# RetNet attention into an ELU feed-forward on one core: four FFN1 tiles pulled into the last attention unit of the start-up, and one weight load issued earlier

## The chip, the cores and the metric

The kernel runs on one core of one Trainium2 chip. The metric is the device time of one execution in microseconds (us); the time of a kernel is the median of its runs. All times inside the kernel are read from one profiled execution.

## The reference, cut to what matters

The input is `q`, `k`, `v` of shape (8 batches, 8 heads, 576 positions, 64) and two weights, `w_in` (512 x 2048) and `w_out` (2048 x 512), all float32.

```python
scores = scale * np.matmul(q, k.transpose(0, 1, 3, 2))
gamma = 1.0 - 2.0 ** (-5.0 - np.arange(H))
Dmat = np.where(rel >= 0, gamma ** rel, 0.0)      # decay with distance, causal; no softmax
attn = np.matmul(scores * Dmat, v)                 # per batch and head
x = attn.transpose(0, 2, 1, 3).reshape(B * S, H * D)   # 4608 tokens x 512
h = x @ w_in                                       # FFN1
g = np.where(h > 0.0, h, np.exp(np.minimum(h, 0.0)) - 1.0)   # ELU
out = g @ w_out                                    # FFN2
```

## The kernel before, in words

The 4608 tokens are cut into 36 units of 128 tokens. Nine units make two sequences, so unit 4 of each nine holds the end of one sequence and the beginning of the next. The decay is split into a factor on the values (`gk`, applied by GpSimd in `scale_v`) and a factor on the output (`gx`, applied by VectorE in `put_x`), so the attention of a unit is a linear recurrence: `turn` transposes queries and keys of the unit on TensorE (8 matmuls against an identity) and copies both halves out of PSUM, one half on VectorE and one on ScalarE; `scores` makes the key-query products; `masks` applies the causal mask on VectorE; `inter` adds the contribution of the state of earlier units; `state` updates that state; `intra` multiplies the masked scores by the values; `put_x` writes the result, transposed, into the tile `xt` that FFN1 reads; `state_out` copies the state for the next unit. `product(u)` is the last five steps in one call.

Units are gathered in groups for the feed-forward part. Group 0 is units 0, 1 and 2 (384 tokens), group 1 is unit 3 alone, and later groups have up to four units (512 tokens). `ffn1(g, ft)` makes a tile of 128 hidden features by the tokens of the group: four matmuls into a PSUM bank (`ph`), then an exponential on ScalarE (`e`, line 336), a subtraction on GpSimd (`m`, line 338), and the ELU on VectorE (`g`, line 315). The last step is held back by three tiles (`late`, `finish`, `tick`) so that VectorE's queue doesn't stand still. A tile of `ph` is free for a later tile when its `g` is written. There are three such banks (`ps_h`), and every fourth tile uses a further one (`ps_m`). `ffn2` and `ffn2_cols` multiply the `g` tiles by `w_out`.

The order of work is written out by hand for the first five units (lines 401 to 493). After that a list of FFN1 and FFN2 steps is interleaved with the attention of later units by due times (lines 496 to 553). Every engine executes its own instructions strictly in the order in which this code issues them.

In the start-up, TensorE also runs dummy matmuls (`dummy(n)`, n matmuls of a zero tile with 512 columns, line 389), whose results nobody reads. Weights are loaded with a cast from float32 to bfloat16 by DMAs that GpSimd's queue issues: `w_in` in four parts of 512 features (`load_w_in(0)` to `load_w_in(3)`, line 105; four FFN1 tiles each), `w_out` as two halves of its first 256 columns (`load_w_out(0, 0, 8)` and `load_w_out(0, 8, 16)`, line 109) and one part for its last 256 columns (`load_w_out(1, 0, 16)`). The queries and keys of each unit come by the same queue (line 94). These GpSimd transfers take eight completion semaphores in turn, so that each waits on its queue for the transfer eight places ahead of it.

The start-up loop before the change:

```python
for u in range(3):
    scores(u)
    inter(u)
    masks(u)
    if u == 0:
        make_gx(1, 2, 3)
    if u < 2:
        dummy(3)
        turn(u + 1, h)
    else:
        dummy(4)
    state(u); intra(u); put_x(u); state_out(u)
    dummy((2, 8, 2)[u])
```

Of the kernel before, what the change touches and what calls it, by code (L numbers as in the profile page):

```python
# [9 lines left out]
FP32 = mybir.dt.float32  # L10
# [7 lines left out]
def kernel(  # L18
# [9 lines left out]
    nc = tc.nc  # L28
# [4 lines left out]
    P = 128  # L33
    HP = H // 2
    KJ = DM // P
# [34 lines left out]
    ps_h = ctx.enter_context(tc.tile_pool(name="ps_h", bufs=3, space=PSUM))  # L70
# [27 lines left out]
    w_in_sb = const.tile([P, KJ, DF], BF16, name="w_in_sb")  # L98
# [8 lines left out]
    def load_w_out(c, f0, f1):  # L107
        s = (slice(None), slice(f0, f1), slice(c * 256, c * 256 + 256))
        nc.gpsimd.dma_start(w_out_sb[s], w_out_v[s])
# [17 lines left out]
    for h in range(H):  # L127
        i = h % 2
# [43 lines left out]
    def scale_v(u):  # L172
        rv = raws[u]
        n = nat.tile([P, H, D], BF16, name="vn", tag="vn")
        nc.gpsimd.tensor_tensor(  # L175
            n, rv, gk[:, u % R].unsqueeze(2).to_broadcast([P, H, D]), ALU.mult
        )
        vns[u] = n

    def turn(u, bank=None):  # L180

        t = tpool.tile([P, 2, HP, P], BF16, name="qkT", tag="qkT")
        n = kns[u]
        if u < PE_TURNED:
            if bank:
                pool, tag = bank
                ps = [pool.tile([P, HP, P], BF16, name="tr", tag=tag) for c in range(2)]
            else:
                both = ps_s.tile([P, 2, 2, HP, P], BF16, name="tr", tag="sc")
                ps = [both[:, c, 0] for c in range(2)]  # L190
            for c in range(2):
                for hp in range(HP):
                    nc.tensor.transpose(ps[c][:, hp], n[:, c, 2 * hp : 2 * hp + 2].rearrange("p h d -> p (h d)"), ident)  # L193
            nc.vector.tensor_copy(t[:, 0], ps[0])
            nc.scalar.copy(t[:, 1], ps[1])  # L195
        else:
            nc.sync.dma_start_transpose(
                t.rearrange("p c h t -> p (c h) t"), n.rearrange("p c h d -> p (c h d)")
            )
        qkTs[u] = t  # L200

    def scores(u):
        t = qkTs[u]
        sc = ps_s.tile([P, 2, HP, P], FP32, name="sc", tag="sc")
        for hp in range(HP):
            for j in range(2):
                for i in range(2):
                    r = slice(i * D, (i + 1) * D)
                    nc.tensor.matmul(  # L209
                        sc[j * 64 : (j + 1) * 64, i, hp], t[r, 1, hp, j * 64 : (j + 1) * 64], t[r, 0, hp],  # L210
                        start=(hp == 0), stop=(hp == HP - 1), skip_group_check=True,
                    )
        scs[u] = sc

    def masks(u, i=None):

        if u not in pts:
            pts[u] = ppool.tile([P, 2, HP, P], BF16, name="pt", tag="pt")
        m = mask[:, 1 if u % R == 4 else 0]
        s = slice(0, 2) if i is None else slice(i, i + 1)  # L220
        nc.vector.tensor_tensor(  # L221
            pts[u][:, s].rearrange("p i h t -> p (i h) t"), scs[u][:, s].rearrange("p i h t -> p (i h) t"),
            m.unsqueeze(1).to_broadcast([P, (s.stop - s.start) * HP, P]), ALU.mult,
        )

    def inter(u):

        o = ps_o.tile([P, HP, P], FP32, name="o", tag="o")
        os_[u] = o
        r = u % R  # L230
        if r == 0:
            return
        n = 64 if r == 4 else P
        for hp in range(HP):
            for i in range(2):
                rows = slice(i * D, (i + 1) * D)
                nc.tensor.matmul(  # L237
                    o[rows, hp, :n], sbs[u][rows, hp], qkTs[u][rows, 0, hp, :n],
                    start=(hp == 0), stop=False, skip_group_check=True,
                )  # L240

    def state(u):

        r = u % R
        if r == 8:
            return
        if r in (0, 4):
            sts[0] = ps_st.tile([P, HP, D], FP32, name="st", tag="st")
        st = sts[0]
        rows = slice(64, P) if r == 4 else slice(0, P)  # L250
        for hp in range(HP):
            for i in range(2):
                h = 2 * hp + i
                nc.tensor.matmul(  # L254
                    st[i * D : (i + 1) * D, hp], kns[u][rows, 1, h], vns[u][rows, h],
                    start=(hp == 0 and r in (0, 4)), stop=(r in (3, 7)), skip_group_check=True,
                )

    def state_out(u):
        if u % R == 8:  # L260
            return
        s = ppool.tile([P, HP, D], BF16, name="sb", tag="sb")
        nc.scalar.copy(s, sts[0])  # L263
        sbs[u + 1] = s

    def intra(u):
        o = os_[u]
        for hp in range(HP):
            for i in range(2):
                h = 2 * hp + i  # L270
                nc.tensor.matmul(  # L271
                    o[i * D : (i + 1) * D, hp], vns[u][:, h], pts[u][:, i, hp],
                    start=(u % R == 0 and hp == 0), stop=(hp == HP - 1), skip_group_check=True,
                )

    xts = {}

    def put_x(u):
        g, i = group_of[u]
        if i == 0:  # L280
            xts[g] = xpool.tile([P, KJ, 512], BF16, name="xt", tag="xt")
        r = u % R
        s0 = P * r if r < 5 else 64 + P * (r - 5)
        nc.vector.tensor_tensor(  # L284
            xts[g][:, :, i * P : (i + 1) * P], os_[u], gx[:, :, s0 : s0 + P], ALU.mult
        )
# [24 lines left out]
    def finish(n=0):  # L311

        while late and late[0][0] <= slot[0] - n:
            _, gt_, ph, m, _ = late.pop(0)
            nc.vector.scalar_tensor_tensor(gt_, ph, 0.0, m, ALU.max, ALU.min)  # L315

    def tick():
        slot[0] += 1
        finish(3)

    def ffn1(g, ft, bank=None):

        n = P * len(GROUPS[g])
        pool, tag = bank or (ps_h, "ph")
        ph = pool.tile([P, 512], FP32, name="ph", tag=tag)
        tiles = 512 // n
        w = slice(0, tiles * n)
        for i in range(tiles):
            f = (ft + i) * P
            for j in range(KJ):  # L330
                nc.tensor.matmul(  # L331
                    ph[:, i * n : (i + 1) * n], w_in_sb[:, j, f : f + P], xts[g][:, j, :n],
                    start=(j == 0), stop=(j == KJ - 1), skip_group_check=True,
                )
        e = epool.tile([P, 512], FP32, name="e", tag="e")
        nc.scalar.activation(e[:, w], ph[:, w], AF.Exp)  # L336
        m = epool.tile([P, 512], BF16, name="m", tag="m")
        nc.gpsimd.tensor_scalar(m[:, w], e[:, w], -1.0, 1.0, ALU.add, ALU.mult)  # L338
        gt_ = gpool.tile([P, 512], BF16, name="g", tag="g")
        late.append((slot[0], gt_[:, w], ph[:, w], m[:, w], (g, ft)))  # L340
        for i in range(tiles):
            gts[g, ft + i] = gt_[:, i * n : (i + 1) * n]
        tick()
# [42 lines left out]
    def dummy(n, bank=(ps_m, "pm")):  # L386
        dum = bank[0].tile([P, 512], FP32, name="dum", tag=bank[1])
        for _ in range(n):
            nc.tensor.matmul(dum, warm[:, :P], warm, start=True, stop=True)  # L389

    def product(u):
        inter(u)
        state(u)
        intra(u)
        put_x(u)
        state_out(u)

    h, m = (ps_h, "ph"), (ps_m, "pm")
# [3 lines left out]
    A(kns[0][:, 0], raw0[0])  # L402
    V(kns[0][:, 1], raw0[1])
    make_gx(0)
    turn(0, h)
    scale_v(0)
    load_w_in(1)
    scale_v(1)
# [4 lines left out]
    load_w_in(3)  # L413
    load_w_out(0, 0, 8)
    load_w_out(0, 8, 16)
    dummy(2)
    for u in range(3):
        scores(u)
        inter(u)
        masks(u)  # L420
        if u == 0:
            make_gx(1, 2, 3)
        if u < 2:
            dummy(3)
            turn(u + 1, h)
        else:
            dummy(4)
        state(u)
        intra(u)
        put_x(u)  # L430
        state_out(u)
        dummy((2, 8, 2)[u])


    def f1(g, n, bank=None):
        k = 512 // (P * len(GROUPS[g]))
        ffn1(g, k * n, bank)

    o = (ps_o, "o")
    for n in range(16):  # L440
        f1(0, n, m if n % 4 == 3 else None)
        if n == 6:
            scale_v(3)
        if n == 7:
            turn(3)
            finish(1)
            dummy(3, o)
            scores(3)
            masks(3, 0)
        if n == 8:  # L450
            masks(3, 1)
        if n == 10:
            product(3)
        if n == 11:
            load_w_out(1, 0, 16)
    for n in range(4):
        f1(1, n, m if n == 3 else None)
        if n == 0:
# [127 lines left out]
```

## Time and profile before

| what | value |
|---|---|
| median of 6 runs | 318.83 us (318.6 to 319.49) |
| profiled execution, its own time | 319.14 us |
| its span, first to last instruction | 317.4 us |
| TensorE busy | 308.8 us (97%) |
| VectorE, ScalarE, GpSimd busy | 54%, 41%, 63% |
| granted TensorE clock | 0.999 |
| bytes read from and written to HBM | 36.70 MB, 9.44 MB |

The profile has one row per engine. In a timeline row the first number is the start in us from the beginning of the span, the second how long the row's instructions lasted together, then the engine (PE is TensorE, DVE VectorE, ACT ScalarE, POOL GpSimd), the line of the code, the operation and the tiles (out<-in), and how many instructions the row merges. Square brackets give the idle time of the engine ahead of the row and what ended it. Matmuls are pipelined: the end of a row overlaps the next row, so the pace is read from start to start.

### The profile page before, as it was taken

Reading aid. Unit: us, or ns where it says so; the run is one execution under the profiler, and the core shown is the slowest. Engines: PE = TensorE matmul, PEld = TensorE weight load, DVE = VectorE, ACT = ScalarE, POOL = GpSimd, SP = SyncE. Lnnn points to the kernel's source line nnn. Section 1 sums busy time; section 2 is a strip of 40 time slices with the busy share of each in tenths; the row PEclk is TensorE's granted clock in tenths of the full one; section 3 lists DMA queues with packets and bytes.
Section 4 is the critical chain, followed back from the end, with each engine's and each line's share of the span. In section 5 each row is a group of like instructions: output and inputs, shape, how many; then the busy total and the mean of one; then the engine's idle time right before and its main releaser. Section 6 shows DMA issues by size and latency. Waiting matters only on the chain.

```text
span 317.4 us, 7528 instructions
## 1 busy us (share of the span) xinstructions
PE 308.8 (97%) x3015; PEld 173.7 (55%) x3015; DVE 172.8 (54%) x279; ACT 131.3 (41%) x243; POOL 200.7 (63%) x288
## 2 busy tenths in 40 slices
PE   8899899999999999999999999999999999999995
PEld 3455888767766555555444444444444444444444
DVE  4557434658666656565566555555555555444300
ACT  4445412444543544344444444344444444344411
POOL 7956885887987777787777666776664433333300
PEclk9999999999999999999999999999999999999999
DMA  9999999997999999999999999999996200000111
GB/s 152 189 208 150 152 191 211 162 194 61 104 143 167 155 135 167 147 128 164 130 147 135 136 133 134 132 135 133 134 132 85 66 35 35 34 33 33 67 68 67
DMA packets 149235, 39.55 MB, mean 125 GB/s; under 512 B 137616, under 2 KB 145168, under 8 KB 149200
## 3 DMA queue, kind: packets, MB, share of 16 engines
q0 software_dynamic: 79264, 13.64, 57.1%
q1 hardware_dynamic: 67920, 23.14, 37.4%
q10 hardware_dynamic: 2016, 2.29, 2.3%
q8 instruction: 23, 0.38, 0.5%
q14 instruction: 12, 0.10, 0.1%
HBM read 36.70 MB, written 9.44 MB: 145 GB/s over the span
## 4 chain that ended last, share of the span: by engine, by line
PE 88%; DVE 4%; POOL 3%; DMA 2%; issue 1%; ACT 1%; POOLq 0%; DVEq 0%; ACTq 0%
PE ph L331 37%; PE pm L356 33%; PE pmh L372 5%; PE sc L209 4%; PE o L271 3%; PE st L254 2%; DMA qkn<-in_k_dram 2%; PE o L237 2%; PE tr L193 2%; DVE pt L221 1%; PE dum L389 1%; POOL m L338 1%; DVE g L315 1%; DVE xt L284 1%; POOL qkn L94 1%
## 5 line engine op out<-in xcount | busy, mean ns | idle before, releaser
L338 POOL TENSOR_SCALAR m<-e 128x512 bf16<-128x512 f32 (+1 forms) x156 | 90.7, 584 | 97.8 <-ACT e L336 95.1
L331 PE MATMUL ph<-xt,w_in_sb 128*128 128x512 bf16 (+3 forms) x832 | 145.7, 314 | 1.4 <-DVE g L315 0.9
L315 DVE SCALAR_TENSOR_TENSOR g<-ph,m 128x512 bf16<-128x512 f32 (+1 forms) x156 | 99.7, 647 | 83.5 <-POOL m L338 82.3
L336 ACT ACTIVATE e<-ph 128x512 f32<-128x512 f32 (+1 forms) x156 | 88.0, 564 | 127.3 <-PE ph L331 126.8
L356 PE MATMUL pm<-w_out_sb,g 128*128 128x512 bf16 x496 | 125.6, 379 | 0.0
L331 PEld LDWEIGHTS <-w_in_sb 128*128 128x128 bf16 x832 | 71.4, 98 | 56.4 <-issue 2.5
L356 PEld LDWEIGHTS <-g 128*128 128x128 bf16 x496 | 47.8, 98 | 53.2 <-issue 0.3
L221 DVE TENSOR_TENSOR pt<-sc,mask 128x1024 bf16<-128x1024 f32 (+1 forms) x37 | 44.0, 1192 | 20.2 <-PE sc L209 19.9
L175 POOL TENSOR_TENSOR vn<-rv,gk 128x512 bf16<-128x512 f32 x36 | 37.5, 1042 | 2.3 <-ACT qkT L195 1.2
L94 POOL DMA_DIRECT2D qkn<-in_q_dram x39 | 35.0, 898 | 0.0
L284 DVE TENSOR_TENSOR xt<-o,gx 128x512 bf16<-128x512 f32 x36 | 24.7, 685 | 16.1 <-PE o L271 16.1
L94 POOL DMA_DIRECT2D qkn<-in_k_dram x39 | 33.3, 856 | 0.1
L363 ACT COPY ot<-pm 128x512 f32<-128x512 f32 x31 | 18.1, 585 | 14.5 <-PE pm L356 14.1
L263 ACT CAST sb<-st 128x256 bf16<-128x256 f32 x32 | 11.9, 372 | 17.2 <-PE st L254 14.4
L372 PE MATMUL pmh<-w_out_sb,g 128*128 128x256 bf16 (+1 forms) x176 | 18.5, 263 | 0.2 <-DVE g L315 0.2
L209 PEld LDWEIGHTS <-qkT 64*64 64x64 bf16 x576 | 9.2, 106 | 14.3 <-issue 11.2
L372 PEld LDWEIGHTS <-g 128*128 128x128 bf16 x176 | 15.7, 98 | 2.3 <-issue 0.4
L209 PE MATMUL sc<-qkT 64*64 64x128 bf16 x576 | 15.0, 222 | 1.0 <-ACT qkT L195 0.7
L271 PE MATMUL o<-pt,vn 128*64 128x128 bf16 x288 | 14.3, 221 | 0.0
L389 PE MATMUL dum<-warm 128*128 128x512 bf16 x39 | 12.5, 458 | 1.2 <-DVE warm L120 1.2
L237 PE MATMUL o<-qkT,sb 64*64 64x128 bf16 (+1 forms) x256 | 12.3, 214 | 0.0
L195 ACT COPY qkT<-tr 128x512 bf16<-128x512 bf16 x12 | 7.0, 585 | 11.0 <-PE tr L193 4.4
(39 smaller groups left out, 80.7 us busy)
## 6 DMA issues: line engine op xcount, KB each, us to landing
rv<-in_v_dram SPq DMA_DIRECT2D x31, 256.0 KB, 5.4
out_dram<-ot SPq DMA_DIRECT2D x27, 256.0 KB, 2.4
qkn<-in_q_dram POOLq DMA_DIRECT2D x31, 128.0 KB, 5.5
qkn<-in_k_dram POOLq DMA_DIRECT2D x31, 128.0 KB, 5.4
w_in_sb<-in_moe_w_in_dram POOLq DMA_DIRECT2D x4, 512.0 KB, 9.8
out_dram<-oth ACTq DMA_DIRECT2D x9, 128.0 KB, 4.8
w_out_sb<-in_moe_w_out_dram POOLq DMA_DIRECT2D x2, 512.0 KB, 14.1
w_out_sb<-in_moe_w_out_dram POOLq DMA_DIRECT2D x1, 1024.0 KB, 10.3
```

The lines of the kernel that those rows point to most:

```text
L94: nc.gpsimd.dma_start(kns[u][p0 : p0 + n, c], (q, k)[c][b, :, s0 : s0 + n, :].rearrange("h p d -> p h d"))
L175: nc.gpsimd.tensor_tensor(n, rv, gk[:, u % R].unsqueeze(2).to_broadcast([P, H, D]), ALU.mult)
L209: nc.tensor.matmul(sc[j * 64 : (j + 1) * 64, i, hp], t[r, 1, hp, j * 64 : (j + 1) * 64], t[r, 0, hp], start=(hp == 0), stop=(hp == HP - 1) ...
L221: nc.vector.tensor_tensor(pts[u][:, s].rearrange("p i h t -> p (i h) t"), scs[u][:, s].rearrange("p i h t -> p (i h) t"), m.unsqueeze(1).t ...
L271: nc.tensor.matmul(o[i * D : (i + 1) * D, hp], vns[u][:, h], pts[u][:, i, hp], start=(u % R == 0 and hp == 0), stop=(hp == HP - 1), skip_g ...
L284: nc.vector.tensor_tensor(xts[g][:, :, i * P : (i + 1) * P], os_[u], gx[:, :, s0 : s0 + P], ALU.mult)
L315: nc.vector.scalar_tensor_tensor(gt_, ph, 0.0, m, ALU.max, ALU.min)
L331: nc.tensor.matmul(ph[:, i * n : (i + 1) * n], w_in_sb[:, j, f : f + P], xts[g][:, j, :n], start=(j == 0), stop=(j == KJ - 1), skip_group_ ...
L336: nc.scalar.activation(e[:, w], ph[:, w], AF.Exp)
L338: nc.gpsimd.tensor_scalar(m[:, w], e[:, w], -1.0, 1.0, ALU.add, ALU.mult)
L356: nc.tensor.matmul(pm, gts[g, ft][:, it * P : (it + 1) * P], w_out_sb[:, ft], start=(ft == 0), stop=(ft == NFT - 1))
L372: nc.tensor.matmul(pm, gts[g, ft][:, it * P : (it + 1) * P], w_out_sb[:, ft, c0:c1], start=(ft == 0), stop=(ft == NFT - 1),)
```

## The change

1. `turn` gets an argument by which VectorE copies the keys and ScalarE the queries, instead of the other way round. Units 0, 1 and 2 use it.
2. `load_w_out(1, 0, 16)`, which was issued after FFN1 tile 11 of group 0, is issued with the other weight loads ahead of FFN1.
3. In the start-up, `inter` of a unit moves behind the turning of the next unit. The dummies between unit 1 and the scores of unit 2 become 2 instead of 8, and the 2 ahead of FFN1 go.
4. The first four FFN1 tiles of group 0 are made in two parts. The part for units 0 and 1 (256 columns) is done around the `product` of unit 2: two tiles ahead of it, two behind. The part for unit 2 (128 columns) follows, and then the rest of each tile's work. Tile 3 takes the `ps_m` bank, as before.
5. In group 0, unit 3 is turned after tile 5 instead of tile 7, its scores stay after tile 7, the three dummies and the forced `finish(1)` between the two go, and `scale_v(3)` moves from after tile 6 to after the scores.

```diff
-    turn(0, h)
+    turn(0, h, True)
...
     load_w_out(0, 8, 16)
+    load_w_out(1, 0, 16)
     dummy(2)
-    for u in range(3):
+    for u in range(2):
         scores(u)
-        inter(u)
         masks(u)
         if u == 0:
             make_gx(1, 2, 3)
-        if u < 2:
-            dummy(3)
-            turn(u + 1, h)
-        else:
-            dummy(4)
-        state(u)
-        intra(u)
-        put_x(u)
-        state_out(u)
-        dummy((2, 8, 2)[u])
+        dummy(3)
+        turn(u + 1, h, True)
+        product(u)
+        dummy(2)
+    scores(2)
+    masks(2)
+    dummy(4)
...
-    for n in range(16):
+    for n in range(2):
+        ffn1_part(0, n, 0, 2)
+    product(2)
+    for n in range(2, 4):
+        ffn1_part(0, n, 0, 2, m if n == 3 else None)
+    for n in range(4):
+        ffn1_part(0, n, 2, 3)
+        f1(0, n)
+    for n in range(4, 16):
         f1(0, n, m if n % 4 == 3 else None)
-        if n == 6:
-            scale_v(3)
+        if n == 5:
+            turn(3)
         if n == 7:
-            turn(3)
-            finish(1)
-            dummy(3, o)
             scores(3)
             masks(3, 0)
+            scale_v(3)
         if n == 8:
             masks(3, 1)
         if n == 10:
             product(3)
-        if n == 11:
-            load_w_out(1, 0, 16)
```

The new function makes the matmuls of one tile for the units u0 to u1 of its group, and `ffn1` picks up the tile from `phs` where it is already made:

```python
def ffn1_part(g, ft, u0, u1, bank=None):
    pool, tag = bank or (ps_h, "ph")
    if (g, ft) not in phs:
        phs[g, ft] = pool.tile([P, 512], FP32, name="ph", tag=tag)
    c = slice(u0 * P, u1 * P)
    for j in range(KJ):
        nc.tensor.matmul(
            phs[g, ft][:, c], w_in_sb[:, j, ft * P : (ft + 1) * P], xts[g][:, j, c],
            start=(j == 0), stop=(j == KJ - 1), skip_group_check=True,
        )
```

More of the change, by code (lines that the diff above doesn't have):

```diff
@@ L178, in scale_v, with turn @@
         vns[u] = n
-    def turn(u, bank=None):
+    def turn(u, bank=None, keys_on_v=False):
         t = tpool.tile([P, 2, HP, P], BF16, name="qkT", tag="qkT")
         n = kns[u]
+        c_v = 1 if keys_on_v else 0
         if u < PE_TURNED:
@@ L193, in turn @@
                     nc.tensor.transpose(ps[c][:, hp], n[:, c, 2 * hp : 2 * hp + 2].rearrange("p h d -> p (h d)"), ident)
-            nc.vector.tensor_copy(t[:, 0], ps[0])
-            nc.scalar.copy(t[:, 1], ps[1])
+            nc.vector.tensor_copy(t[:, c_v], ps[c_v])
+            nc.scalar.copy(t[:, 1 - c_v], ps[1 - c_v])
         else:
@@ L319, in tick @@
         finish(3)
+    phs = {}
+    def ffn1_part(g, ft, u0, u1, bank=None):
+        pool, tag = bank or (ps_h, "ph")
+        if (g, ft) not in phs:
+            phs[g, ft] = pool.tile([P, 512], FP32, name="ph", tag=tag)
+        c = slice(u0 * P, u1 * P)
+        for j in range(KJ):
+            nc.tensor.matmul(
+                phs[g, ft][:, c], w_in_sb[:, j, ft * P : (ft + 1) * P], xts[g][:, j, c],
+                start=(j == 0), stop=(j == KJ - 1), skip_group_check=True,
+            )
     def ffn1(g, ft, bank=None):
         n = P * len(GROUPS[g])
-        pool, tag = bank or (ps_h, "ph")
-        ph = pool.tile([P, 512], FP32, name="ph", tag=tag)
         tiles = 512 // n
         w = slice(0, tiles * n)
[L328 to L334, printed above, removed]
+        if (g, ft) in phs:
+            ph = phs.pop((g, ft))
+        else:
+            pool, tag = bank or (ps_h, "ph")
+            ph = pool.tile([P, 512], FP32, name="ph", tag=tag)
+            for i in range(tiles):
+                f = (ft + i) * P
+                for j in range(KJ):
+                    nc.tensor.matmul(
+                        ph[:, i * n : (i + 1) * n], w_in_sb[:, j, f : f + P], xts[g][:, j, :n],
+                        start=(j == 0), stop=(j == KJ - 1), skip_group_check=True,
+                    )
         e = epool.tile([P, 512], FP32, name="e", tag="e")
```

## The prediction

> **What bounds the kernel now.** I read the page first, then the waits of TensorE, then its timeline over the start-up, then GpSimd's timeline and the landing times of single transfers.
>
> ```profile
> PE 308.8 (97%) x3015; PEld 173.7 (55%) x3015; DVE 172.8 (54%) x279; ACT 131.3 (41%) x243; POOL 200.7 (63%) x288
> PEclk9999999999999999999999999999999999999999
> DMA  9999999997999999999999999999996200000111
> ```
>
> TensorE is the bound. Split by stretches, it is busy for 254.20 of the 255.00 us from 57 to 312 us, and its waits there sum to 0.4 us. So a microsecond that TensorE saves before 57 us should come out at the end whole, provided that no load becomes late. The waits from 0 to 80 us and the chain's start show what can be saved:
>
> ```profile
> PE tr L193 <- DMA qkn<-in_k_dram: 1.3, 1, 1.3
> PE ph L331 <- DVE g L315: 0.9, 1, 0.9
> PE sc L209 <- ACT qkT L195: 0.7, 2, 0.5
> PE ph L331 <- DVE xt L284: 0.2, 1, 0.2
> ```
>
> ```profile
> 12.98 0.61 PE L193 MATMUL tr<-ident,qkn 128*128 128x128 bf16 x8
> ...
> 13.99 1.90 PE L389 MATMUL dum<-warm 128*128 128x512 bf16 x8
> 15.82 0.42 PE L209 MATMUL sc<-qkT 64*64 64x128 bf16 x16
> ...
> 17.92 0.61 PE L389 MATMUL dum<-warm 128*128 128x512 bf16 x2
> 18.77 5.36 PE L331 MATMUL ph<-xt,w_in_sb 128*128 128x384 bf16 x32 [0.24 <-DVE xt L284]
> 23.96 0.61 PE L193 MATMUL tr<-ident,qkn 128*128 128x128 bf16 x8
> 24.41 0.81 PE L389 MATMUL dum<-warm 128*128 128x512 bf16 x3
> 25.71 0.42 PE L209 MATMUL sc<-qkT 64*64 64x128 bf16 x16 [0.49 <-ACT qkT L195]
> ...
> 33.29 3.73 PE L331 MATMUL ph<-xt,w_in_sb 128*128 128x128 bf16 x64 [0.91 <-DVE g L315]
> ```
>
> The reader sees TensorE filling time with dummies that cover waits (8 at 13.99, 2 at 17.92, 3 at 24.41), two waits beside them, and 0.91 us at 33.29, whose cause stands in GpSimd's timeline: the issue of the last `w_out` part, in front of four `m`.
>
> ```profile
> 30.87 1.22 POOL L109 DMA_DIRECT2D w_out_sb<-in_moe_w_out_dram  x1
> 32.12 1.94 POOL L338 TENSOR_SCALAR m<-e 128x384 bf16<-128x384 f32 x4
> ```
>
> **The change part by part.** Paces from start to start: a dummy 0.216 us, an FFN1 matmul of 384 columns 0.162 us (a tile 0.65), of 256 columns 0.109 us (8 in 1.04 us of which the last one's tail is 0.17, at 71.65), of 128 columns 0.056 us.
>
> *Up to the scores of unit 2.* The swap of the copies would free unit 0's scores some 0.16 us earlier (ACT's copy takes 0.59 us, DVE's 0.42), but TensorE then waits until 10.25 us for unit 1's keys in both kernels: worth nothing; had the keys landed sooner, 0.16. With `inter(1)` moved behind it, `turn(2)` starts at about 12.6 instead of 12.98, and there meets a transfer: unit 2's keys were issued at 4.81 and landed 8.3 us later, at 13.1. So TensorE waits about 0.35 us in the middle of that turning. The keys are turned by 13.4, `product(1)` costs 0.81 to 0.9 us (28.11 to 28.92 for unit 3's), two dummies 0.43, and the scores start at 14.8, not 15.82. The six dummies removed are 1.30 us, of which 0.3 goes to the new wait and to one more change of matmul shape. Gain: 1.00.
>
> *Up to FFN1's start.* Scores and four dummies last until 16.05. `w_in(0)` was issued at 5.67 and landed 10.0 us later, at 15.7, so it is there, by 0.4 us; `put_x(1)` ends about 15.1. Two partial tiles (8 x 0.109) run to 16.9, `product(2)` to 17.8 (its mask is done at 16.5, 0.47 + 1.22 us after the scores), two more to 18.7. `put_x(2)` starts 0.26 us after the last `intra` and takes 0.69, so it ends at 18.65: it now lies under the partial tiles. The 1.74 us of FFN1 done by 18.7 put the equivalent start at 16.96, 2.14 us after the scores; it was 2.95. Gain: 0.80, which is two dummies and the wait for `xt`.
>
> *The burst.* This is what takes most of it back. The four 128-column parts last 0.22 us each, so four tiles are finished at 19.6, and all four banks are full. Tile 4 needs `g` of tile 0. Before, tile 0's last matmul was issued by 19.41, `e` began at 19.61, `m` at 20.19, `g` at 20.73 and ended at 21.28: 1.87 us. Now tile 0 is complete at 18.92, so its `g` ends at 20.79 and tile 4 starts at 20.84: TensorE stands still for 1.24 us. Behind it the chain frees a bank every 0.48 us (four `m` in 1.94), faster than the 0.65 of a tile, so it is one stall. Queued behind tile 4 are tile 5 and unit 3's turning, which are delayed with it. Loss: 1.24.
>
> *The load moved ahead.* In the order of the built instructions the last `w_out` part is the 14th GpSimd transfer in both kernels, and waits for the semaphore of the 6th, `w_in(1)`, issued at 8.65 and landed 9.7 us later, at 18.35. In the old place this cost nothing. In the new place GpSimd stands still from 17.56 to 18.35, then issues for 1.22 us: free at 19.57. The first `m` is due at 19.70, so it is hidden by 0.13 us only; each 0.1 us of landing later than 18.5 is 0.1 us more of stall. Bounds for the issue itself: 1.22 (its own row) and 1.79 (both halves of the other columns together), so 0 to 0.45 us; I take 0, by its own row. At the old place the wait of 0.91 us goes (1.07 us by starts, 32.22 to 33.29). What is late next there is `g` of tile 12, at about 30.4, when TensorE arrives at 30.45, so no new wait. Gain: 1.07. The transfer itself now directly follows the other halves, whose second landed at 32.2; the DMA engines are nearly idle from 30 to 33 us, so it should land about 39, and its first reader comes at 44.2 − 2.8 = 41.4. The halves are first read at about 34. If the transfer were late, those microseconds come off one for one. Queries and keys of units 4 and 5 keep their place behind it in the queue; SP's queue gets nothing new.
>
> *Unit 3.* Turning after tile 5 starts at 22.1; its transfers were issued at 10.53 and 11.47 and landed by 20.1. The copies are done by about 23.2, behind `e` of tile 5, and the scores come after tile 7 at 24.0: 1.30 us (24.41 to 25.71) of dummies and waiting go, less 0.1 for one more change of shape. `scale_v(3)`, one GpSimd operation of 1.04 us, now starts behind tile 7's `m` at 25.2 and ends at 26.2; `state(3)` reads it at 26.7, and the `m` of tiles 8 and 9 queued behind it free banks that TensorE wants only at 27.9. The `w_in` parts landed at 23.2 and 25.7; tiles 8 and 12 read them at 24.3 and 27.9. VectorE's two half masks before `g` of tiles 6 and 7 leave tile 10's bank free at 25.6 when wanted at 25.65, tight. Gain: 1.2.
>
> *Sum:* 1.00 + 0.80 − 1.24 + 1.07 + 1.2 = 2.83 us.
>
> **Two rules against this change.** First, granted clock: the twelve dummies at the start step by 0.427 us, the later ones by 0.216, and the clock record begins with 1.00 at 6.3 us. TensorE's longest pause since, 1.25 us at 10.25, left it there. The Trainium skill (TensorE: Matmul & The Clock Gate, HAM oscillation — how this bites in real kernels) says that pauses over about 3.4 us throttle it to half. The new pauses (0.35, 1.24) are shorter, so the row's answer is 0 loss; were a window of 3.4 us run at half pace, the loss would be 1.7 and the sum 1.1. Second, narrower matmuls: the same page (Back-to-back issue gap) gives about 81 ns for each weight load with a 128-column matmul. The trace has 64 in 3.57 us (33.29 to 36.86), 56 ns. By the rule the sixteen 128-column matmuls cost 0.4 us more, sum 2.4; I go by the row.
>
> **The rivals.**
>
> *GpSimd is held by the moved load: slower.* GpSimd writes the descriptors of its transfers into rings of limited room (the Trainium skill, DMA: Bandwidth & Descriptors, SWDGE vs HWDGE vs iDMA, has them in a part of SBUF; no row here shows how much they hold). If those of 1024 KB don't fit behind seven transfers in flight, GpSimd waits, and all sixteen `m` with it. For it: in the old place nearly everything earlier had landed. Against it: the second half at 16.65 also had seven in flight ahead of it and took its usual 0.9 us. It decides once GpSimd is free later than 19.70 + 2.83 = 22.5. Held until `w_in(2)` lands at 23.16, it issues to 24.4; TensorE is 4.7 us later, net 1.9 slower: 320.7.
>
> *The gain is given back to the transfers.* The DMA tenths read 9 until 238 us. Were loads the pace in there, the early microseconds would turn to waits: 318.8. Against: TensorE waits 0.4 us in all after 57 us, and no wait there names a load.
>
> *The clock drops once:* 317.7, as above.
>
> *The stall is smaller,* because keys or the chain come sooner than I place them: up to 3.6 us gained, 315.2.
>
> **How the numbers follow.** The profiled execution took 319.14 us, 1.74 over its span; 319.14 − 2.83 = 316.31. The median is 0.31 lower: 318.83 − 2.83 = 316.0. Forecast 0.72 (own range 315.4 to 316.9, for the tight places at 19.57, 25.6 and 41.4), smaller stall 0.10, clock 0.05, given back 0.05, GpSimd held 0.08. Faster: 0.87; no change 0.05; slower 0.08. About 0.2%, 0.6 us, is what this measurement can tell from no change. The range of 8 in 10 goes from 315.2 to 317.3.
>
> **What would show it.** Right: scores of unit 2 near 14.8 with a wait of 0.3 on its keys; no dummies after 16; one wait of about 1.2 us of `ph` for `g` near 20.8; `w_out` issued near 18.3 on GpSimd; group 1 starting near 30.4, not 33.29; nothing new after 41. Wrong: `m` starting after 19.8, a wait of `pmh` for `w_out` near 41, or half-pace matmuls after 20.

## The result and the profile after

The changed kernel takes 317.25 us (median of 16 executions, 315.62 to 318.66), the kernel before 319.09 (34 executions). The ratio is 0.9934, with a 95% interval from 0.9917 to 0.9951: 2.1 us faster by the ratio (1.6 to 2.6). The forecast was 316.0 in a range of 315.2 to 317.3. The direction held and the median lies inside the range, but only 0.05 us from its upper end; the forecast gain of 2.83 us lies outside the interval. The executions spread over 3 us where those of the kernel before mostly keep within 1.

The profiled execution took 318.24 us over a span of 316.5, so it is one of the long ones, and it shows two things that the sum did not have. The page's clock row, and TensorE's longest wait (in all, times, longest):

```profile
PEclk9998999999999999999999999999999999999999
...
PE ph L349 <- DVE g L316: 2.0, 1, 2.0
```

The wait of `ph` for `g` is the stall of the burst, forecast at 1.24 us and here 1.96. The clock row has an 8 in its fourth slice. TensorE's timeline around it:

```profile
11.97 0.87 PE L194 MATMUL tr<-ident,qkn 128*128 128x128 bf16 x8
...
14.12 0.42 PE L210 MATMUL sc<-qkT 64*64 64x128 bf16 x16
14.47 1.04 PE L407 MATMUL dum<-warm 128*128 128x512 bf16 x4
15.35 1.04 PE L331 MATMUL ph<-xt,w_in_sb 128*128 128x256 bf16 x8
...
17.13 1.94 PE L331 MATMUL ph<-xt,w_in_sb 128*128 128x256 bf16 x24
21.03 1.57 PE L349 MATMUL ph<-xt,w_in_sb 128*128 128x384 bf16 x8 [1.96 <-DVE g L316]
22.39 1.06 PE L194 MATMUL tr<-ident,qkn 128*128 128x128 bf16 x8
23.24 2.66 PE L349 MATMUL ph<-xt,w_in_sb 128*128 128x384 bf16 x8
25.83 0.42 PE L210 MATMUL sc<-qkT 64*64 64x128 bf16 x16
```

The order of steps is the forecast one. The two lines after 22.3 are at half pace: eight matmuls of 384 columns from 23.24 take 2.59 us to the next line, where the kernel before needs 1.30. The view by windows gives, for each stretch, its length, each engine's busy time with the number of its instructions (TensorE first), and the granted clock in its third number from the right:

```profile
15.35:18.93 3.58, 3.58 (x57) 3.03 (x56) 1.16 (x2) 0.87 (x3) 1.74 (x3) 1.00 1.77 204
18.93:22.25 3.32, 1.36 (x11) 0.78 (x9) 1.83 (x4) 1.46 (x4) 2.84 (x5) 1.00 1.22 207
22.25:25.66 3.41, 3.41 (x18) 1.92 (x16) 1.48 (x4) 1.74 (x4) 1.29 (x3) 0.50 1.32 206
25.66:29.06 3.40, 3.40 (x54) 1.97 (x52) 2.68 (x5) 2.08 (x5) 2.74 (x6) 1.00 1.45 195
```

One window of 3.41 us runs at 0.50, directly behind a stretch in which TensorE was busy for 1.36 of 3.32 us. The clock record of this execution begins at 5.18 us, and 5.18 + 5 x 3.413 = 22.25: the clock changes only at the edges of windows of 3.413 us that follow one another. In the profile of before the record begins at 6.33 us, in the others at 3.98 to 7.19, so where the windows fall in the program differs from one execution to the next.

GpSimd's timeline shows why the stall was longer than the chain alone makes it:

```profile
15.06 1.79 POOL L109 DMA_DIRECT2D w_out_sb<-in_moe_w_out_dram  x2
18.69 1.15 POOL L109 DMA_DIRECT2D w_out_sb<-in_moe_w_out_dram  x1 [1.84 <-DMA w_in_sb<-in_moe_w_in_dram]
19.86 1.94 POOL L356 TENSOR_SCALAR m<-e 128x384 bf16<-128x384 f32 x4
```

The moved load waits for `w_in(1)`, as read from the order of instructions, and is issued from 18.69. The `e` of tile 0 began at 18.43, so its `m` was due at 19.01 (18.43 + 0.58) and started at 19.86: 0.85 us of this execution's stall is this load, and 1.96 − 0.85 = 1.11 the burst.

The mean clock of an execution tells whether it had such a window: 3.4 of 316 us at half pace make a mean of 0.9946. Of the changed kernel, 7 of 16 executions have a mean of 0.995 or less, with a median of 317.96; the other 9 have a median of 316.54. Of all executions of the kernel before that ran beside the experiments, 14 of 59 have such a mean, with a median of 320.66; the other 45 have 319.09. At full clock the change is therefore worth 319.09 − 316.54 = 2.55 us, give or take a few tenths: the nine executions go from 315.62 to 318.28.

### The profile page after: what moved, and what is told of

The parts are those of the page before. It is cut to its first block, busy times and chain, and to the rows that moved or that the text cites. A ratio compares the mean times of both kernels' runs of the same rounds, so it can differ in the third digit from the quotient of the medians.

```text
span 316.5 us, 7538 instructions
## 1 busy us (share of the span) xinstructions
PE 307.6 (97%) x3020; PEld 174.1 (55%) x3020; DVE 172.8 (55%) x279; ACT 131.0 (41%) x243; POOL 200.6 (63%) x288
## 4 chain that ended last, share of the span: by engine, by line
PE 89%; DVE 3%; DMA 3%; POOL 2%; issue 1%; ACT 0%; DVEq 0%; POOLq 0%; ACTq 0%
PE ph L349 38%; PE pm L374 33%; PE pmh L390 5%; PE sc L210 4%; DMA w_in_sb<-in_moe_w_in_dram 3%; PE o L272 3%; PE st L255 2%; PE o L238 2%; PE tr L194 2%; PE dum L407 1%; DVE pt L222 1%; DVE g L316 1%; DVE xt L285 1%; POOL qkn L94 1%; POOL m L356 1%
## 5 line engine op out<-in xcount | busy, mean ns | idle before, releaser
L349 PEld LDWEIGHTS <-w_in_sb 128*128 128x128 bf16 x816 | 70.3, 98 | 56.2 <-issue 3.9
L395 DVE COPY oth<-pmh 128x256 f32<-128x256 f32 (+1 forms) x6 | 2.4, 402 | 16.2 <-PE pmh L390 16.2
```

What stands on the lines that cost most here:

```text
L349: nc.tensor.matmul(ph[:, i * n : (i + 1) * n], w_in_sb[:, j, f : f + P], xts[g][:, j, :n], start=(j == 0), stop=(j == KJ - 1), skip_group_ ...
```

## The experiments

Each kernel was run beside the kernel before on the same chip. In this list "at full clock" means executions with a mean clock of 0.998 or more.

**1. Only the load moved.** In the kernel before:

```diff
     load_w_out(0, 8, 16)
+    load_w_out(1, 0, 16)
...
-        if n == 11:
-            load_w_out(1, 0, 16)
```

> The kernel before with its last w_out load issued ahead of FFN1, nothing else changed. Theory 1 (in the old place the issue of 1.22 us delayed four m and TensorE 1.07 us at 33.3): GpSimd is free at about 19.8, m of tile 0 is due at 20.2, so nothing is lost in the new place, and the time falls by 1.07 us, ratio 0.9966. Theory 2 (that wait only moves to the next place where GpSimd is late): no change. Theory 3 (the hold in the new place reaches tile 4): gain of 0.3 to 0.8 us.

Measured: ratio 0.9958 (0.9942 to 0.9973), median 318.07, all 8 executions at full clock: 1.01 us below 319.09. The wait of 0.91 us at 33.29 is gone, and FFN1 runs without a break into group 1 and to FFN2:

```profile
28.91 7.04 PE L331 MATMUL ph<-xt,w_in_sb 128*128 128x384 bf16 x84
35.78 0.49 PE L372 MATMUL pmh<-w_out_sb,g 128*128 128x256 bf16 x3
```

The term of 1.07 us is right. In this profile the load was issued at 19.01 in its new place, behind `w_in(1)`, and held the first `m` only 0.13 us (20.17 instead of 20.04), for which TensorE did not wait: without the early tiles that `m` is due later.

**2. Only unit 3.** In the kernel before:

```diff
-        if n == 6:
+        if n == 5:
-            scale_v(3)
+            turn(3)
         if n == 7:
-            turn(3)
-            finish(1)
-            dummy(3, o)
             scores(3)
             masks(3, 0)
+            scale_v(3)
```

> The kernel before with the change's fifth part alone: unit 3 turned after tile 5, no dummies and no forced finish before its scores, scale_v(3) behind them. Theory 1 (1.30 us of dummies and waiting at 24.4 go): at full clock 1.1 to 1.3 us faster, ratio 0.9960 to 0.9966; scores of unit 3 without a wait. Theory 2 (the dummies and the wait covered something that is late next): under 0.5 us faster.

Measured: ratio 0.9961 (0.9940 to 0.9983); at full clock 317.89 (10 of 12 executions), 1.20 us below. The scores of unit 3 come without a wait, and the load's wait stays, as it should:

```profile
23.37 0.61 PE L193 MATMUL tr<-ident,qkn 128*128 128x128 bf16 x8
23.81 1.46 PE L331 MATMUL ph<-xt,w_in_sb 128*128 128x384 bf16 x8
25.21 0.42 PE L209 MATMUL sc<-qkT 64*64 64x128 bf16 x16
...
32.81 1.39 PE L331 MATMUL ph<-xt,w_in_sb 128*128 128x128 bf16 x22 [0.91 <-DVE g L315]
```

The term of 1.2 us is right.

**3. Only the early part:** the swapped copies, the order and dummies of the start-up, and the four early tiles. In the changed kernel:

```diff
-    load_w_out(1, 0, 16)
...
-        if n == 5:
-            turn(3)
+        if n == 6:
+            scale_v(3)
         if n == 7:
+            turn(3)
+            finish(1)
+            dummy(3, o)
...
-            scale_v(3)
...
+        if n == 11:
+            load_w_out(1, 0, 16)
```

> The kernel before with the change's first, third and fourth part alone: order and dummies of the start-up and the four early tiles; the w_out load and unit 3 stay where they were. Theory 1 (1.00 up to unit 2's scores, 0.80 up to FFN1, 1.24 lost in the stall): at full clock 0.4 to 0.9 us faster, a stall of 1.0 to 1.3 us at tile 4 with m of tile 0 starting 0.6 us after its e, and more executions at half clock than the kernel before has. Theory 2 (the stall is the load's fault and not the burst's): no stall, 1.8 us faster.

Measured: ratio 0.9978 (0.9956 to 0.9999); at full clock 318.44 (10 of 12), 0.65 us below. The burst stalls TensorE by itself:

```profile
17.32 1.94 PE L331 MATMUL ph<-xt,w_in_sb 128*128 128x256 bf16 x24
20.37 2.76 PE L349 MATMUL ph<-xt,w_in_sb 128*128 128x384 bf16 x16 [1.10 <-DVE g L316]
```

and `m` starts at 19.21, 0.58 us after its `e` at 18.63. The sum 1.00 + 0.80 − 1.24 = 0.56 agrees with it as a net; its three terms were not timed apart, but the stall's 1.24 is 1.10 here. The interval of this ratio reaches from no gain to 1.4 us. The three parts alone make 1.01 + 1.20 + 0.65 = 2.86 us, where the forecast had 2.83; together they make 2.55 at full clock. The difference of 0.3 us is what one would expect if the load lengthens the stall in some executions, but it is not clear of the noise of four medians.

**4. The load behind the fourth tile.** In the changed kernel:

```diff
-    load_w_out(1, 0, 16)
...
     for n in range(4):
         ffn1_part(0, n, 2, 3)
         f1(0, n)
+    load_w_out(1, 0, 16)
```

> The changed kernel with the last w_out load issued behind the m of the fourth FFN1 tile instead of ahead of FFN1. Theory 1 (GpSimd is held by this load until w_in(1) has landed, and m of tile 0 starts at 19.86 instead of 0.58 us after its e at 18.43): the load is issued behind four m, at about 21; the stall falls from 1.96 to about 1.2 us, and with fewer executions at half clock the median falls by 0.7 to 1.3 us. Theory 2 (GpSimd's hold is beside the chain, as forecast): no change. Theory 3 (the load now delays m of tile 4, due at about 21.5, by 0.6 us and that reaches tile 8): gain under 0.3 us.

Measured: median 316.83 (6 executions, one of them at half clock for a window), ratio 0.9918 (0.9896 to 0.9940). Its profile has what theory 1 says, the load issued at 22.29 behind four `m`, and a stall of 1.10 us. But its median at full clock, 316.70, is not below the 316.54 of the changed kernel. By this run alone the gain is not shown; in its profile unit 1's keys were turned from 10.57 us instead of 9.63, which moves everything behind them.

**5. The stall filled.** Behind the four early tiles of the changed kernel, `dummy(5, o)`.

> The changed kernel with five dummies (5 x 0.216 = 1.08 us) behind the four early FFN1 tiles, inside the stall of 1.96 us that the profile shows there, so that TensorE has work in it. Theory 1 (the spread of the changed kernel, 315.6 to 318.7 us, comes from the clock: a window of 3.4 us that holds the whole stall puts TensorE at half pace for the next one, 1.7 us): the stall's idle time falls below 1 us, no window of half clock follows in any execution, and the median goes from 317.25 to 316.0 to 316.6, with the executions close together. Theory 2 (the spread comes from when transfers land, and the dummies only fill time): same median, same spread. Theory 3 (the dummies delay tile 4): about 1 us slower.

Measured: median 316.41, ratio 0.9924 (0.9897 to 0.9952); 2 of 6 executions still have a half-clock window (318.05 and 318.11), the others 316.07 to 316.43. So the dummies cost nothing, and theory 1 fails as put: the clock halves in some executions though the stall is filled.

**6. No partial tiles.** The kernel of experiment 4, with `product(2)` first and four whole tiles behind it in place of the partial ones.

> As the kernel with the load behind the fourth tile, and without the partial tiles: product(2) comes first and the four tiles are made whole behind it. Theory 1 (the partial tiles buy 0.8 us and the burst at their end pays 1.2 to 2 us back): FFN1 starts about 2.95 us after the scores of unit 2, no stall at tile 4, and the time is 0.3 to 0.6 us below the kernel with the load moved alone, with no execution at half clock: about 315.8. Theory 2 (the early tiles are worth their 0.8 us): 0.5 to 0.8 us slower than the kernel with the load moved alone.

Measured: median 316.93, ratio 0.9916 (0.9891 to 0.9942). There is no stall at tile 4, and yet 3 of 6 executions have a half-clock window. At full clock the median of three is 315.94. A place that experiments 5 and 6 share with the changed kernel is the wait for unit 1's keys at about 8.5 to 10 us; the next experiments try it.

**7. That wait made emptier, in the kernel before:** no dummies ahead of unit 1's turning.

```diff
         if u < 2:
-            dummy(3)
+            if u:
+                dummy(3)
             turn(u + 1, h)
```

> The kernel before without the three dummies ahead of unit 1's turning; they lie ahead of a wait of 0.9 to 1.5 us for that unit's keys, so at full clock nothing changes but the length of that wait. Theory 1 (a window of 3.4 us with the array busy for under some two fifths is followed by half clock): the window around the keys' wait falls from about 0.42 busy to about 0.25; executions with a mean clock under 0.998 go from 6 of 36 to over half, each 1.4 to 1.7 us longer than those at full clock, whose median stays at 319.1. Theory 2 (half-clock windows come from something other than this place): the share stays at a sixth and the median at 319.1.

Measured: 6 of 12 executions have a half-clock window; median of these 320.37, of the others 319.34. One of the six, at 322.23 us, has a mean of 0.989, which is two such windows. The kernel before, run beside it, has 8 of 23. Six of 12 against 8 of 23 are too few to tell apart, so this experiment doesn't show that emptying the wait raises the share. "Over half" was too high, and the cost, 1.0 us, too low for the expectation.

**8. That wait filled, in the changed kernel:**

```diff
-        dummy(3)
+        dummy(3 if u else 8)
         turn(u + 1, h, True)
```

> The changed kernel with eight instead of three dummies ahead of unit 1's turning, nothing else; the stall behind the four early tiles stays empty. Theory 1a (both places drop the clock): fewer executions under 0.998 than 7 of 16, not none; full-clock median near 316.5. Theory 1b (it is the keys' wait alone): none, median 316.5. Theory 1c (it is the stall alone): share as before, about 4 of 10.

Measured: no half-clock window, where the kernel before has 8 of 23 beside it. One of its six executions took 796 us, which no other run repeats, and is left out here; the other five have a median of 316.41 (316.31 to 317.46); the ratio is 0.9901 (0.9868 to 0.9933). The stall is still there and empty:

```profile
7.95 1.90 PE L407 MATMUL dum<-warm 128*128 128x512 bf16 x8
9.69 0.88 PE L194 MATMUL tr<-ident,qkn 128*128 128x128 bf16 x8
...
20.77 1.46 PE L349 MATMUL ph<-xt,w_in_sb 128*128 128x384 bf16 x8 [1.13 <-DVE g L316]
```

The load is in the same place as in the change, and yet this stall has the length of the burst alone. GpSimd is free of the load at 19.59, which is 0.59 us after the `e` of tile 0 at 19.00: here the margin just sufficed.

```profile
18.43 1.15 POOL L109 DMA_DIRECT2D w_out_sb<-in_moe_w_out_dram  x1 [0.86 <-DMA w_in_sb<-in_moe_w_in_dram]
19.59 1.94 POOL L356 TENSOR_SCALAR m<-e 128x384 bf16<-128x384 f32 x4
```

In this execution unit 1's keys landed at 10.12 us, nearly as in the profile of before (10.20), and no window was lost. So it is the forecast's own case, and the gain comes out as forecast. The same scores row, here and in the kernel before, are 57.37 − 54.55 = 2.82 us apart:

```profile
54.55 0.42 PE L210 MATMUL sc<-qkT 64*64 64x128 bf16 x16 [0.24 <-DVE rv L83]
```

```profile
57.37 0.42 PE L209 MATMUL sc<-qkT 64*64 64x128 bf16 x16 [0.24 <-DVE rv L83]
```

**9. Both places filled, load as in the change:** experiment 8 with `dummy(4, o)` behind the four early tiles.

> The changed kernel with both places filled (five dummies more ahead of unit 1's turning, four in the stall) and its w_out load left ahead of FFN1. Theory 1 (the early load holds GpSimd until w_in(1) has landed and lengthens the stall): no execution at half clock, and 0.2 to 0.6 us slower than the kernel with both places filled and the load behind the fourth tile (316.33): 316.5 to 316.9. Theory 2 (the hold is beside the chain): same, 316.2 to 316.4.

Measured: none of 12 executions has a half-clock window; median 316.70, ratio 0.9922 (0.9897 to 0.9947). Five of the twelve take 318.06 to 319.05 all the same, and the profile caught one of them. GpSimd's timeline:

```profile
16.11 1.04 POOL L175 TENSOR_TENSOR vn<-rv,gk 128x512 bf16<-128x512 f32 x1 [2.46 <-DMA rv<-in_v_dram]
17.10 1.57 POOL L105 DMA_DIRECT2D w_in_sb<-in_moe_w_in_dram  x2
18.64 2.93 POOL L109 DMA_DIRECT2D w_out_sb<-in_moe_w_out_dram  x3
21.54 1.98 POOL L356 TENSOR_SCALAR m<-e 128x384 bf16<-128x384 f32 x4
```

Here unit 2's values landed 3 us later than in the profile of before, GpSimd stood at `scale_v(2)` for them, and every load behind it was late. With the third `w_out` part in that queue, the first `m` starts at 21.54 (the `e` of tile 0 at 19.36), and TensorE's stall is 1.90 us long behind four dummies:

```profile
19.83 1.03 PE L407 MATMUL dum<-warm 128*128 128x512 bf16 x4
22.76 1.46 PE L349 MATMUL ph<-xt,w_in_sb 128*128 128x384 bf16 x8 [1.90 <-DVE g L316]
```

**10. Both filled, load behind the fourth tile.**

> The changed kernel with its w_out load behind the fourth tile, four dummies in the stall behind the four early tiles, and eight instead of three dummies ahead of the turning of unit 1, so that the wait for that unit's keys is filled too (five more, 1.08 us, against a wait of 1.1 to 1.5). Theory 1 (half-clock windows follow from a window of 3.4 us in which the array is busy for less than some two fifths; in the changed kernel there are two such places, the wait for unit 1's keys and the stall): no execution at half clock, all within about 0.6 us of each other apart from transfers, median 315.8 to 316.4. Theory 2 (the half-clock executions have another cause, as with the stall alone filled, where 2 of 6 still had them): 2 or more of 6 stay near 318. Theory 3 (the added dummies delay the turning): 0.3 us or more slower than 316.5 in all.

Measured: no half-clock window in 6; median 316.33 (five at 316.19 to 316.44, one at 317.65), ratio 0.9901 (0.9870 to 0.9932). Against experiment 9 the median is 0.37 us lower. That is not clear of noise: the two ran on different chips, the intervals of their ratios overlap, and without the five executions above 318 experiment 9 has a median of 316.45. What those five share was seen in one profile only.

**11. Both filled, no partial tiles,** with two dummies in the wait for `xt`.

> As the kernel with both places filled, but without the partial tiles: product(2), two dummies in the wait for xt, then four whole tiles. Theory 1: no execution at half clock, and as there is no burst, the same time as with partial tiles or 0.3 to 0.8 us below it: 315.4 to 316. Theory 2 (the partial tiles are worth their 0.8 us): 316.5 to 317.

Measured: no half-clock window in 6; median 316.25 (315.81 to 316.83), ratio 0.9893 (0.9863 to 0.9923). It is the lowest median of all kernels, and not told apart from experiment 10: with the load behind the fourth tile, no gain from the partial tiles can be seen.

**12. Unit 3 turned in the stall:** experiment 10 with `dummy(3, o)` and `turn(3)` there, instead of behind tile 5.

> The kernel with both places filled and the w_out load behind the fourth tile, with unit 3's turning (0.45 us of TensorE) moved from behind tile 5 into the stall, behind three dummies. Theory 1 (the stall is TensorE time that useful work can take, and unit 3's keys land at about 20.4): 0.2 to 0.45 us faster than 316.33: 315.9 to 316.1, no execution at half clock. Theory 2 (the turning waits for the keys and then delays tile 4, or its copy on VectorE delays the g of tiles 2 and 3): same or up to 0.3 us slower.

Measured: no half-clock window in 6; median 316.45, ratio 0.9898 (0.9869 to 0.9928): no gain over 316.33, within the spread. In its profile the turning runs in the stall, from 20.61, and tile 4 follows at 21.23, where experiment 10 had the same distance without it: 3.04 us from the third early tile's start (18.19 and 17.57) to tile 4 in one and 3.05 in the other. From the third early tile to FFN2 it is 16.10 us (to 34.29) against 16.28 (to 33.85). So of the 0.45 us of the turning 0.18 is left, and in this execution unit 2's keys landed 0.62 us later (13.46 against 12.84), which took more than that.

## Why the prediction was right, and where it was not

*TensorE bound, early savings kept:* right. The gains of the three parts alone appear at the end of a run of 319 us with the size that they have at 33 us, and experiment 8 has 2.82 us at 57 us and a median 2.68 us below 319.09.

*The terms of the sum:* right by experiments 1 to 3, within a few tenths: 1.07 against 1.01, 1.2 against 1.20, and 0.56 for the early part as a whole against 0.65. The new wait for unit 2's keys, put at 0.35, is 0.27 to 0.52 in the five profiles whose rows show it.

*"The first `m` is due at 19.70, so it is hidden by 0.13 us only":* this step failed. The time of the first `m` was worked out from one execution in which unit 1's keys landed at 10.2 us. In the profile after they landed at 9.6, so TensorE and `e` came 0.7 us earlier, while `w_in(1)` landed at 18.41 as before, and GpSimd resumed only 0.28 us after that. A cover of 0.13 us between two engines that hang on different transfers is no cover. It cost 0.85 us in the profiled execution and nothing in that of experiment 8. What it costs in the median stays open: 2.86 for the parts against 2.55 together and 0.37 between experiments 9 and 10 point to about 0.3 us, but experiment 4, which takes the load away, is at full clock not faster than the change (316.70 against 316.54). The rival of a held GpSimd named another cause, room for descriptors, and that one did not come: the 1024 KB behind seven transfers in flight were issued in 1.15 us. What held GpSimd is the wait for `w_in(1)` that the forecast itself had counted.

*The signs of being wrong* that the forecast named: two of three are in the profile of the change, an `m` after 19.8 (19.86) and half-pace matmuls after 20 (from 22.25). So the number lies in the range, but the profiled execution is not the one that was forecast.

*"The row's answer is 0 loss" for the clock:* this is the larger miss, by its frequency. It was given 0.05; 7 of 16 executions of the changed kernel have it, at 1.4 us each (median 317.96, where the forecast had 317.7 for this case), and so had 14 of 59 of the kernel before, which its profile does not show, since that execution was not one of them. That the median stayed in the range is in part luck: had two more of the 16 lost a window, it would be about 317.46 (estimate: the middle of 317.30 and 317.62, the next two in order), outside the range. The rule weighed there (the Trainium skill, TensorE: Matmul & The Clock Gate, HAM oscillation — how this bites in real kernels) asks for a pause of some 3.4 us; the longest pause in the profile after is 1.96, and the clock halved. By the rule the loss is 0, by the row 1.7 us in such an execution; the measurement decides. What fits the traces is a share of work per window: columns streamed times 0.42 ns (0.216 us for 512) fill 0.37 of the window from 18.83 to 22.25 us, which was followed by half clock. The ends of the programs give more such windows, at no cost, since TensorE has nothing left to do. Experiment 5 is one; its last matmul leaves a pause of 2.04 us to the window's edge:

```profile
309.67:313.09 3.42, 1.38 (x25) 1.20 (x22) 0.35 (x2) 0.27 (x1) 0.00 (x0) 1.00 0.26 82
313.09:314.30 1.21, 0.00 (x0) 0.00 (x0) 0.00 (x0) 0.00 (x0) 0.00 (x0) 0.50 0.00 0
```

Over all the profiles, half clock followed the six windows with a share of up to 0.37 (0.12 to 0.34 at five ends of programs), and none with 0.39 (experiment 9) or more (0.41 and 0.43 at the ends of experiments 11 and 7). The same windows are sorted as well by the longest pause inside them, 1.96 us and more against 1.90 and less. So a pause well under 3.4 us suffices, but which of the two counts is not shown, and a single matmul of 384 columns is 0.05 of a window.

*Which place drops the clock:* kernels with the keys' wait filled (experiments 8 to 12) have no half-clock window in 35 executions. With it unfilled, the changed start-up (the change and experiments 3 to 6) has 15 in 46 and the kernel before 14 in 59. So filling this wait, which was in both kernels from the start, takes the half-clock windows away, and it is the likely main place. It is inferred from these counts alone: no kept profile shows a half-clock window behind this wait, and the least share of a window over it is 0.56 (experiment 3). That the stall can do it too is shown by one profile, of the change itself; experiment 8 leaves the stall empty and has no such window in five, which is too few to say how often. Whether the change raised the share at all (7 of 16 against 14 of 59) the counts don't settle.

*The second rule weighed,* 81 ns for a matmul of 128 columns with its weights: the sixteen early ones run at the trace's pace. From the first of 256 columns at 17.13 to the last of 128 at 18.85, the 23 steps take 1.72 us; 8 x 0.109 + 15 x 0.056 = 1.71.

## What to carry to other kernels

Work put ahead to fill a wait pays only until its consumers' buffers are full: four tiles finished together are worth what the chain behind them takes in, and here whole tiles later did as well. An issue on a queue is free where its engine waits for nothing else; look up which earlier transfer its semaphore belongs to, and take a margin of less than the landing times' spread (here 1.2 us for one transfer) for none. Before a start-up is tuned by one profile, look at the mean clock of all executions: one that loses a window of full clock hides gains of the same size.

## What the runs showed of the hardware that was not expected

In the profile of the change the clock halved for one window of 3.413 us behind a window in which the array was about 0.37 busy by columns, though no pause was longer than 1.96 us; behind windows at 0.39 or more it never did in the kept profiles. The edges of the windows lie 3.413 us apart and fall anywhere relative to the program. The landing of one and the same first transfers moves between executions: unit 1's keys from 9.6 to 10.7 us, unit 2's values from 11.8 to 16.0.
